# Third unit's h by twenty block products, with w_in's sums made ahead of it

## The chip, the core and the metric

The kernel runs on one core of one Trainium2 chip. The metric is the time of one execution in microseconds (us) on the device. Three runs of the kernel before took 576.93, 576.26 and 574.91 us; the median is 576.26 us. Another execution, taken with the profiler, gave the trace that everything below is read from.

## What is computed

The reference is a gated linear attention over 4 batches, 8 heads, 768 tokens and 48 channels, followed by a two-layer MLP on its output:

```python
for t in range(S):
    state = f[:, :, t, :, None] * state + np.einsum('bhd,bhe->bhde', k[:, :, t], v[:, :, t])
    y[:, :, t] = np.einsum('bhd,bhde->bhe', q[:, :, t], state)
...
x = attn_out.transpose(0, 2, 1, 3).reshape(B * S, H * D)     # 3072 x 384
h = x @ w_in                                                  # 3072 x 2048
g = h * (1.0 / (1.0 + np.exp(-1.702 * h)))
out = g @ w_out                                               # 3072 x 384
```

f is the sigmoid of f_logit. The weights arrive as 64-bit floats and are converted on the chip to 32-bit ones.

## The kernel before

The tokens are cut into twelve units of 256 tokens (n = 0 to 11, three per batch). Each unit goes through attention and then through the MLP. TensorE (PE) works on both at once: a list named fill holds the MLP's matmuls of earlier units, and a plan says after which part of a unit's attention how many of them are issued.

**Attention of a unit.** VectorE (DVE) turns f, q and k into the layout that is needed (turn, line 382; reads raw). GpSimd (POOL) makes products of the decays in a tree (begin_gates, line 457, tile tot; its first one must wait until the states of the unit before have been read from tot). There are six levels: PE makes scores (tile sc, line 466), DVE multiplies the keys and queries X by decays (promote, line 564), ScalarE (ACT) sets copies aside (Kc and Qc, lines 535 and 541), DVE and ACT move the scores out of PSUM into A (lines 507, 516, 526). Two levels share one sc tile, in levels(0), levels(2) and levels(4). Part S adds A times v (line 584), makes the state updates on PE (line 695) and chains the states on DVE (lines 717 to 721, tile st). Part W adds queries times states (line 742), copies y out (yT, line 757) and sends it by DMA to xT (lines 815 and 820), the MLP's input.

**The MLP of a unit, plain form** (mlp_h, line 1173; mlp_o, line 1187). Units 0 and 1 use it in blocks of four of the sixteen 128-row slices of w_in: per slice three matmuls of 128x128 by 128x256, then the activation on ACT; then matmuls with w_out. DVE sums the blocks (line 1243).

**The twenty-product form** (mlp_h20, line 1042). Units 3 to 11 use it. w_in and the unit's x are cut into blocks, and h comes from twenty products of sums of w_in's blocks (WA) by sums of x's blocks (E), four matmuls of 128x128 by 128x128 each (line 1079), in the order WHOLE. The sums of x, twelve, are made on POOL by sums_of_x (line 1037) from xT, after part W. The sums of w_in are made once: some into tiles of their own (sums_of_w, line 1000, names c1, c2, c3, c4, p4, p6, p12, p15, p16), nine in place over w_in's blocks (sums_in_place: k and p3, p1, p14, p7, p19, p9, p5, p11). DVE adds products that meet in one block of h (line 1107), ACT copies (lines 1086, 1098) and activates (1094, 1109). The w_out side of units 2 to 11 is a scheme of seven products on PE (mlp_o7, line 937; results o_Y, o_W, o_X, o_Z) that uses sums of w_out's quarters, T[1] to T[4] (line 851, DVE), and sums of g (lines 872 to 881, DVE).

**Unit 2 before** has h in the plain form, 48 matmuls of 256 columns in groups of four slices, last group first. After each group, when its slices of w_in are read, sums_in_place(r) overwrites blocks of w_in. So w_in's sums are complete only for unit 3.

**What sets the order.** Up to unit 2's attention every engine's order is the program's own (manual_schedule over all engines, closed by fill_order.close()); after it only PE and POOL keep it, and a scheduler orders DVE, ACT and SP, held back where issue_after names an instruction. PLAN and HOLES are strings of steps run after each part of units 1 to 3, or inside a level: f issues the next item of fill, c one step of a weight's conversion (lines 241, 248, 251), p begins a conversion (ACT, line 252), w fetches a pair of weight slices by DMA from SP, s runs one of chores, a list of sums, and k is a matmul that does nothing. From unit 4 on merge shares out the fill. xT tiles and the sums E rotate through three buffers of one tag.

Some deciding lines of the kernel before:

```python
if n > N_FILL:                      # N_FILL = 2
    sums_of_x(n)
...
if n > N_FILL:
    return mlp_h20(n, g, before) + o
...
for r in reversed(range(NGR)):
    items += mlp_h(n, range(r * FG, (r + 1) * FG), by_block)
    if r:
        items.append((0, lambda r=r: sums_in_place(r), 0))
```

Of the kernel before, what the change touches and what calls it, by code (L numbers as in the profile page):

```python
# [23 lines left out]
def kernel(  # L24
# [248 lines left out]
            state["done"] += 2  # L273


    HOLES = {(N_FILL, 0): "c", (N_FILL, 1): "cccffcfcw", (N_FILL, 2): "fcp", (N_FILL, 3): "cfcf", (N_FILL, 4): "fcwwff", (N_FILL, 5): "c"}

    def convert_in(n, l):

# [73 lines left out]
    def attention(n):  # L353
# [19 lines left out]
        def turn(j, outs, fn=None, pieces=None):  # L373

            if n >= N_FILL and not (n == N_FILL and j in BY_PE):
                for f in (1, 0):
                    out = outs(f)
                    at, step = (0, 1) if f else (HALF - 1, -1)
                    with ExitStack() as order:
                        if j == 2 and f == 0 and n % 2 == 0 and "sum" in copied:  # L380
                            order.enter_context(tc.issue_after(copied["sum"].ins))
                        copied["turned"] = nc.vector.transpose(  # L382
                            view(out, at, [[HALF, NP], [step, R4], [R4 * step, 32]]),
                            by_half[:, j, f].rearrange("p a (j d) -> p (a j) d", j=R4)[:, :, :32],
                        )
# [339 lines left out]
        def _():  # L725
# [101 lines left out]


    HF, HC = NFF // 2, DM // 2
    T = {}  # L830
# [4 lines left out]
    def sums_of_b():  # L835
# [9 lines left out]
        made = count()  # L845
# [37 lines left out]
    def mlp_o7(n, g):  # L883
        a = lambda i, j: lambda f: g[j][:, f, i * G:(i + 1) * G]
        s = lambda i: lambda f: g["S"][:, f, i * G:(i + 1) * G]
        b = lambda i, j: lambda f: quarter(w_out, i, j)[:, f]
        T_ = lambda i: lambda f: T[i][:, f] if i < 4 else T[4](f)
        t = {}
        left, right = slice(0, HC), slice(HC, DM)

# [83 lines left out]
    def sums_of_w(names):  # L974

        for name in names:
            if name == "p16":
                WA[name] = wp.tile([P, 2 * DM], F32, tag="s", name="N_p16", bufs=1)[:, :FG * P]
            else:
                WA[name] = const.tile([P, FG * P], F32, name=f"N_{name}")  # L980
            WA[name] = WA[name].rearrange("p (t x) -> p t x", x=2 * P)
        first = (
            ("c3", "a30", "", "a32"), ("p15", "a21", "+", "a31"), ("c2", "a11", "+", "a12"), ("p6", "c2", "+", "a22"),
            ("p6", "p6", "", "c3"),
        )
        second = (
            ("c1", "a01", "+", "a02"), ("c4", "a02", "", "a00"), ("p12", "a11", "", "c4"), ("p4", "c1", "-", "a30"),
            ("p12", "p12", "+", "a10"), ("p16", "a20", "", "a21"), ("p12", "p12", "+", "a20"), ("p16", "p16", "", "a22"),
            ("p15", "p15", "", "p4"),
        )  # L990
        for out, x, op, y in first if "c3" in names else second:
            yield lambda x=(out, x, op, y): sum_of_w(nc.vector if x[2] == "-" else nc.gpsimd, *x)

    def sum_of_w(engine, out, x, op, y):

        if op == "-":
            with tc.issue_after(copied["promoted"].ins):
                engine.scalar_tensor_tensor(WA[out], WA[x], -1.0, WA[y], op0=ALU.mult, op1=ALU.subtract)
        else:
            engine.tensor_tensor(WA[out], WA[x], WA[y], ALU.add if op else ALU.subtract)  # L1000

    def sums_in_place(r):

        while chores:
            chores.pop(0)()
        pool, ve = nc.gpsimd, nc.vector
        for engine, out, at, x, op, y in {
            3: (
                (pool, "k", "a02", "a02", "+", "a30"), (pool, "p3", "a02", "a11", "", "k"), (ve, "p7", "a01", "a11", "", "c3"),
                (ve, "p11", "a00", "a00", "", "c1"),  # L1010
            ),
            2: (
                (pool, "p14", "a10", "a10", "", "c2"), (ve, "p19", "a12", "c2", "-", "a20"), (ve, "p9", "a11", "c4", "", "a11"),
            ),
            1: ((pool, "p1", "a32", "a21", "+", "c3"), (ve, "p5", "a31", "a31", "", "c3")),
        }[r]:
            WA[out] = WA[at]
            sum_of_w(engine, out, x, op, y)

    def sums_of_x(n):  # L1020

# [20 lines left out]
    def mlp_h20(n, g, before):  # L1042
# [68 lines left out]
        def begin():  # L1111
            for half in range(2):
                g[half] = g_tile(f"g_{n}_{half}", width(n))
            free = lanes["o"]
# [44 lines left out]
    def mlp_h(n, ffs, g):  # L1159
        t = {}  # L1160

        def one(ff, c):
            if c == 0:
                if ff % FG == 0:

                    if not halves:
                        new = g_tile(f"g_{n}_{ff}")
                        halves.extend((new[:, :FG], new[:, FG:]))
                        g["tile", ff // HF] = new
                    g[ff // FG] = halves.pop(0 if n < N_FILL else -1)  # L1170
                t["ph"] = bank([P, U], f"h_{n}_{ff}")
            ph = t["ph"]
            nc.tensor.matmul(  # L1173
# [26 lines left out]
    def mlp_unit(n, fill):  # L1200
# [15 lines left out]
        by_block = {}  # L1216

        def end():

            g[0], g[1] = (by_block["tile", i] for i in range(2))  # L1220
            sums_of_a(n, g)
            lanes["o"] = [next(turns) % 4 for _ in range(4)]
        items = []
        for r in reversed(range(NGR)):
            items += mlp_h(n, range(r * FG, (r + 1) * FG), by_block)
            if r:
                items.append((0, lambda r=r: sums_in_place(r), 0))
        return items + [(0, end, 0)] + o

    sums = {}  # L1230

# [92 lines left out]
    def follow_steps(steps):  # L1324

        for step in steps:
# [7 lines left out]
            elif step == "w":  # L1334
                fetch_weights()
            elif step == "s":
                for job in chores[:1]:
                    chores.remove(job)
                    job()
# [21 lines left out]
    def opening():  # L1361
# [16 lines left out]
        load_v(0)  # L1378
        load_raw(1, 1)
        fetch_weights()  # L1380
        for l in range(NL):
            chosen[:] = [2, 3][l % 2:][:1]
            level(l)
# [12 lines left out]
        for l in range(NL - 1):  # L1396
            evacuate(l)
            if l == 1:
                units[0][3]()
                fetch_weights()  # L1400
        chosen[:] = [2, 3, 2, 3]
        next_q()
        begin_pair(1)
# [4 lines left out]
        for _ in range(NOP):  # L1408
# [5 lines left out]
    FIRST = 'k'  # L1414
    PLAN = {
        3: (
            "ffffffsfffsfff", "fffsf", "ffffs", "fffsfsfssfffff", "s", "f", "ffsffffff", "ffffffffff", "fffffsssf",
        ),
        1: (
            "cccwcccwkkkkk", "kkkcf", "cfccwf", "fcffcwffcffcf", "ffcc", "f", "cwc", "fcc", "ff", "cff", "", "f",  # L1420
            "wffwfffff",
        ),
        2: (
            "ffffff", "fcfff", "fcffffccswfwpfcsf", "cfc", "ccfcffscsffcf", "ffffsffffffff", "f", "fffcffsffff",
        ),
    }
    fill += mlp_blocks((0, 0)) + mlp_blocks((0, 1))
# [8 lines left out]
    while chores:  # L1436
        chores.pop(0)()
# [12 lines left out]
    
# [34 lines left out]
```

## Time and profile before

| | before |
|---|---|
| median of three runs | 576.26 us |
| the profiled execution: its time, its span | 575.35 us, 573.6 us |
| mean granted TensorE clock | 1.000 |
| PE, PEld busy | 563.7, 516.7 us |
| DVE, ACT, POOL busy | 441.2, 291.7, 144.5 us |
| share of PE in the chain that ended last | 90% |

The span runs from the first to the last instruction; 1.75 us of the profiled execution lie around it. PE counts matmuls and PEld weight loads, which overlap. Every 32-bit matmul of the program stands in the trace as two matmuls, so unit 2's 48 matmuls are 96 records. The ends of matmuls are modelled, so this text takes the time of a matmul from one start to the next. A line of the timeline has the start, the time to the end of the merged group, engine, line, operation and tiles, the count, and in brackets the idle time ahead and what ended it.

### The profile page before, as it was taken

To read this page: it belongs to the slowest core of one execution; us is meant where nothing else is said; L and a number is where in the kernel's file an instruction comes from. 1 tells how busy PE (TensorE), PEld (TensorE's weight loads), DVE (VectorE), ACT (ScalarE), POOL (GpSimd) and SP (SyncE) were. 2 spreads that over 40 slices of the span, in tenths; PEclk is the share of its full clock that TensorE was granted. 3 is DMA by queue.
4 is the path that set the end of the run, shared out by engine and by line. 5 is a ranking of instruction groups with operands and counts; after the bars stand their busy time and mean duration, and the time that the engine had idled before them with its cause. 6 is when DMAs were issued, how large, how long until landed. Compare 5 with 4: busy or idle time off the path is not lost.

```text
span 573.6 us, 18612 instructions
## 1 busy us (share of the span) xinstructions
PE 563.7 (98%) x7876; PEld 516.7 (90%) x7876; DVE 441.2 (77%) x695; ACT 291.7 (51%) x592; POOL 144.5 (25%) x227
## 2 busy tenths in 40 slices
PE   8899999999999999999999999999999999999997
PEld 7767777786899999999999999999999999999996
DVE  2899688988997786887887888886888886462294
ACT  4755553432553573564564564564564573543440
POOL 4030220419451601601601601601501601303000
PEclk9999999999999999999999999999999999999999
DMA  7869595932362452363453353453362121001000
GB/s 180 207 183 228 138 261 133 246 79 77 84 163 68 120 139 57 85 172 76 109 129 71 97 130 88 113 127 71 97 158 44 49 57 30 30 2 29 29 1 28
DMA packets 85939, 60.01 MB, mean 105 GB/s; under 512 B 33441, under 2 KB 77633, under 8 KB 85857
## 3 DMA queue, kind: packets, MB, share of 16 engines
q1 hardware_dynamic: 85328, 58.21, 40.3%
q8 instruction: 62, 1.02, 0.8%
q10 hardware_dynamic: 529, 0.62, 0.4%
q14 instruction: 20, 0.16, 0.1%
HBM read 45.16 MB, written 8.91 MB: 94 GB/s over the span
## 4 chain that ended last, share of the span: by engine, by line
PE 90%; DMA 3%; DVE 2%; ACT 2%; issue 1%; SPq 1%; ACTq 0%; DVEq 0%
PE h L1079 28%; PE o_Y L937 14%; PE o_Z L937 9%; PE h L1173 9%; PE sc L466 6%; PE o L1187 6%; PE o_X L937 5%; PE o_W L937 4%; PE y L584 2%; PE y L742 2%; PE t L394 2%; PE sc L695 2%; DMA xT<-yT 1%; DVE X L564 1%; DMA bits<-in_moe_w_in_dram 1%
## 5 line engine op out<-in xcount | busy, mean ns | idle before, releaser
L564 DVE TENSOR_TENSOR X<-X,tot 128x1024 f32<-128x1024 f32 x50 | 69.0, 1381 | 40.7 <-PE sc L466 35.1
L535 ACT COPY Kc<-X 128x512 f32<-128x512 f32 x72 | 48.3, 671 | 85.6 <-DVE X L564 71.0
L1079 PE MATMUL h<-E,w_in 128*128 128x128 f32 (+1 forms) x648 | 82.6, 276 | 0.0
L1079 PEld LDWEIGHTS h<-E,w_in 128*128 128x128 f32 x648 | 77.1, 192 | 0.5
L1107 DVE TENSOR_TENSOR g<-g,h 128x512 f32<-128x512 f32 (+1 forms) x92 | 55.4, 628 | 25.9 <-PE h L1079 18.0
L1037 POOL TENSOR_TENSOR E<-xT 128x128 f32<-128x128 f32 (+1 forms) x36 | 16.0, 454 | 231.0 <-DMA xT<-yT 231.0
L1173 PE MATMUL h<-xT,w_in 128*128 128x256 f32 x288 | 65.6, 382 | 0.2 <-DMA xT<-yT 0.2
L1173 PEld LDWEIGHTS h<-xT,w_in 128*128 128x128 f32 x288 | 53.8, 190 | 9.3 <-DMA xT<-yT 0.6
L1109 ACT ACTIVATE g<-g 128x512 f32<-128x512 f32 (+1 forms) x70 | 40.3, 588 | 34.1 <-DVE g L1107 34.1
L937 PE MATMUL o_Y<-T,S 128*128 128x192 f32 x320 | 57.6, 329 | 0.0
L937 PEld LDWEIGHTS o_Y<-T,S 128*128 128x128 f32 x320 | 52.3, 190 | 0.5
L1187 PE MATMUL o<-w_out,g 128*128 128x384 f32 x128 | 44.3, 492 | 0.0
L1098 ACT ACTIVATE g<-h 128x512 f32<-128x512 f32 (+1 forms) x70 | 37.0, 550 | 12.9 <-PE h L1079 11.0
L382 DVE STREAM_TRANSPOSE X<-raw 128x512 f32<-128x512 f32 x38 | 40.9, 1115 | 1.5 <-PE y L742 1.0
L526 DVE COPY_PREDICATED A<-masks,sc 128x256 f32<-128x256 uint32 (+1 forms) x98 | 41.9, 503 | 0.0
L757 ACT COPY yT<-y 48x256 f32<-48x256 f32 (+1 forms) x66 | 22.0, 369 | 30.0 <-PE y L742 29.5
L1079 PE MATMUL h<-E,N_c 128*128 128x128 f32 (+1 forms) x288 | 37.1, 275 | 0.0
L1187 PEld LDWEIGHTS o<-w_out,g 128*128 128x128 f32 x128 | 23.6, 190 | 14.6 <-issue 0.7
L1079 PEld LDWEIGHTS h<-E,N_c 128*128 128x128 f32 x288 | 35.1, 192 | 0.2 <-DVE osb L897 0.2
L466 PE MATMUL sc<-X,Kc 48*64 48x64 f32 x1344 | 28.3, 220 | 3.0 <-ACT Kc L535 1.2
L1177 ACT ACTIVATE g<-h 128x256 f32<-128x256 f32 x48 | 17.7, 382 | 25.5 <-PE h L1173 25.2
L466 PEld LDWEIGHTS sc<-X,Kc 48*64 48x64 f32 x1344 | 24.1, 134 | 7.3 <-ACT Kc L535 3.1
(132 smaller groups left out, 1103.4 us busy)
## 6 DMA issues: line engine op xcount, KB each, us to landing
bits<-in_moe_w_out_dram SPq DMA_DIRECT2D x8, 768.0 KB
raw<-in_f_logit_dram SPq DMA_DIRECT2D x48, 96.0 KB
raw<-in_k_dram SPq DMA_DIRECT2D x48, 96.0 KB
bits<-in_moe_w_in_dram SPq DMA_DIRECT2D x8, 576.0 KB
raw<-in_q_dram SPq DMA_DIRECT2D x44, 96.0 KB
k_tok<-z SPq DMA_DIRECT2D x64, 64.0 KB
kt<-k_tok SPq DMA_DIRECT2D x16, 256.0 KB
out_dram<-osb SPq DMA_DIRECT2D x20, 192.0 KB
```

Of the source, the lines that this page charges most:

```text
L382: copied["turned"] = nc.vector.transpose(view(out, at, [[HALF, NP], [step, R4], [R4 * step, 32]]), by_half[:, j, f].rearrange("p a (j d) - ...
L466: nc.tensor.matmul(t["sc"][h][g * HS:(g + 1) * HS, a, s, :], lhsT=t["Kc", l][rows(h), x:x + HS], rhs=rhs(h, a, g), start=True, stop=True,)
L526: moved = nc.vector.copy_predicated(out=view(A, c * HALF + at, dims), mask=mask.bitcast(U32), data=got)
L535: nc.scalar.copy(c.rearrange("p (n two m) -> p n two m", two=2, m=m), view(X, KF * SLOT, [[2 * m, SLOT // (2 * m)], [(KR - KF) * SLOT + m, ...
L564: done = nc.vector.tensor_tensor(x, x, y, ALU.mult)
L937: nc.tensor.matmul(t[name], lhsT=lhs(f), rhs=rhs(f), start=(new and i == 0), stop=(i == HF - 1), skip_group_check=True,)
L1079: nc.tensor.matmul(ph[:, t], lhsT=WA[a][:, f // 2, f % 2 * P:(f % 2 + 1) * P], rhs=E[n][b], start=(root and t == 0), stop=not goes_on, ski ...
L1098: nc.scalar.activation(to, ph, AF.Copy, scale=float(sign))
L1107: copied["sum"] = nc.vector.tensor_tensor(to, to, part, ALU.add if sign > 0 else ALU.subtract)
L1109: nc.scalar.activation(to, to, AF.Gelu_apprx_sigmoid)
L1173: nc.tensor.matmul(ph, lhsT=w_in[:, ff // 2, c, ff % 2 * P:(ff % 2 + 1) * P], rhs=xTs[n][:, c, :], start=(c == 0), stop=(c == NK - 1))
L1187: nc.tensor.matmul(t["po"], lhsT=g[ff // FG][:, ff % FG, tt * P:(tt + 1) * P], rhs=w_out[:, ff, :], start=(ff == ffs[0]), stop=(ff == ffs[ ...
```

## The change

Unit 2's h is made by the twenty products as well. For that:

- sums_of_x is called for every unit that reaches it: unit 2, and unit 0 too, for which nothing reads them. (Unit 1 returns ahead of that line.)
- All of w_in's sums must stand ahead of unit 2's h. The sums c1, c4 and p12 follow the first five on POOL within unit 2's plan. Four in place (k, p3, p1, p14) go to POOL and five (p7, p19, p9, p5, p11) to DVE. p4 (DVE) and p15's last step (POOL) come behind these, p16's two steps (POOL) behind unit 2's sums of x.
- The sums T of w_out no longer wait for the turn of unit 3's k.
- The plans of units 1 to 3 and HOLES are laid anew. In PE's order, unit 2's sc of levels 2 and 3 comes ahead of five w_out matmuls of unit 1 instead of behind them, part W of unit 2 ahead of three w_out matmuls, 24 instead of 34 of unit 2's w_out matmuls lie between part W of unit 3 and unit 3's first product, and the rest of the order hardly differs. The opening's DMA order is the same; the DMA of weight pair 9 goes ahead of unit 2's v, that of pair 11 behind unit 3's f_logit.

```diff
-    HOLES = {(N_FILL, 0): "c", (N_FILL, 1): "cccffcfcw", (N_FILL, 2): "fcp", (N_FILL, 3): "cfcf", (N_FILL, 4): "fcwwff", (N_FILL, 5): "c"}
+    HOLES = {(N_FILL, 0): "ccc", (N_FILL, 1): "c", (N_FILL, 3): "cpccfwwff", (N_FILL, 4): "ccsw", (N_FILL, 5): "f"}
...
-            if n > N_FILL:
-                sums_of_x(n)
+            sums_of_x(n)
...
         def sub(*x):
-            with ExitStack() as order:
-                if next(made) < 2:
-                    order.enter_context(tc.issue_after(copied["turned"].ins))
-                nc.vector.tensor_tensor(*x, ALU.subtract)
+            summed.append(nc.vector.tensor_tensor(*x, ALU.subtract))
...
-        if op == "-":
-            with tc.issue_after(copied["promoted"].ins):
+        with ExitStack() as order:
+            if engine == nc.vector:
+                order.enter_context(tc.issue_after(copied.get("promoted", copied["state"]).ins))
+            if op == "-":
                 engine.scalar_tensor_tensor(WA[out], WA[x], -1.0, WA[y], op0=ALU.mult, op1=ALU.subtract)
+            else:
+                engine.tensor_tensor(WA[out], WA[x], WA[y], ALU.add if op else ALU.subtract)
...
+    def sums_in_place(engine):
+
+        if engine == nc.gpsimd:
+            for out, at in (("p7", "a01"), ("p19", "a12"), ("p5", "a31"), ("p9", "a11"), ("p11", "a00")):
+                WA[out] = WA[at]
+            sums = (
+                ("k", "a02", "a02", "+", "a30"), ("p3", "a02", "a11", "", "k"), ("p1", "a32", "a21", "+", "c3"),
+                ("p14", "a10", "a10", "", "c2"),
+            )
         else:
-            engine.tensor_tensor(WA[out], WA[x], WA[y], ALU.add if op else ALU.subtract)
...
+            sums = (
+                ("p7", "a01", "a11", "", "c3"), ("p19", "a12", "c2", "-", "a20"), ("p9", "a11", "c4", "", "a11"),
+                ("p5", "a31", "a31", "", "c3"), ("p11", "a00", "a00", "", "c1"),
+            )
...
-        if n > N_FILL:
-            return mlp_h20(n, g, before) + o
...
+        return mlp_h20(n, g, before) + o
...
     chores += [*sums_of_w(("c3", "p15", "c2", "p6"))]
+    more = [lambda: sums_of_w(("c1", "c4", "p12")), lambda: sums_of_w(("p4", "p16"))]
     follow(2, fill, PLAN[2])
...
-    while chores:
-        chores.pop(0)()
+    by_pool, by_ve, rest = [*sums_in_place(nc.gpsimd)], [*sums_in_place(nc.vector)], [*more.pop()()]
+    for x in (*by_pool, *by_ve[:2], *rest[:2]):
+        x()
...
-    of_b = [*sums_of_b()]
-    for x in sums_of_w(("c1", "c4", "p12", "p4", "p16")):
-        chores += of_b[:1] + [x]
-        del of_b[:1]
-    chores += of_b
+    chores += by_ve[2:] + rest[2:] + [*sums_of_b()]
     follow(3, fill, PLAN[3])
```

More of the change, by code (lines that the diff above doesn't have):

```diff
@@ L381, in turn @@
                             order.enter_context(tc.issue_after(copied["sum"].ins))
-                        copied["turned"] = nc.vector.transpose(
+                        nc.vector.transpose(
                             view(out, at, [[HALF, NP], [step, R4], [R4 * step, 32]]),
@@ L829 @@
     HF, HC = NFF // 2, DM // 2
-    T = {}
+    T, summed = {}, []
     def quarter(w, i, j, ffs=slice(0, HF)):
@@ L886, in mlp_o7, with T_, block @@
         b = lambda i, j: lambda f: quarter(w_out, i, j)[:, f]
-        T_ = lambda i: lambda f: T[i][:, f] if i < 4 else T[4](f)
+        def T_(i):
+            def block(f):
+                assert len(summed) == 8
+                return T[i][:, f] if i < 4 else T[4](f)
+            return block
         t = {}
@@ L986, in sums_of_w @@
         second = (
-            ("c1", "a01", "+", "a02"), ("c4", "a02", "", "a00"), ("p12", "a11", "", "c4"), ("p4", "c1", "-", "a30"),
-            ("p12", "p12", "+", "a10"), ("p16", "a20", "", "a21"), ("p12", "p12", "+", "a20"), ("p16", "p16", "", "a22"),
-            ("p15", "p15", "", "p4"),
-        )
-        for out, x, op, y in first if "c3" in names else second:
+            ("c1", "a01", "+", "a02"), ("c4", "a02", "", "a00"), ("p12", "a11", "", "c4"),
+            ("p12", "p12", "+", "a10"), ("p12", "p12", "+", "a20"),
+        )
@@ L992, in sums_of_w @@
+        third = ("p4", "c1", "-", "a30"), ("p15", "p15", "", "p4"), ("p16", "a20", "", "a21"), ("p16", "p16", "", "a22")
+        for out, x, op, y in first if "c3" in names else third if "p16" in names else second:
             yield lambda x=(out, x, op, y): sum_of_w(nc.vector if x[2] == "-" else nc.gpsimd, *x)
     def sum_of_w(engine, out, x, op, y):
-        if op == "-":
-            with tc.issue_after(copied["promoted"].ins):
+        with ExitStack() as order:
+            if engine == nc.vector:
+                order.enter_context(tc.issue_after(copied.get("promoted", copied["state"]).ins))
+            if op == "-":
@@ L998, in sum_of_w @@
                 engine.scalar_tensor_tensor(WA[out], WA[x], -1.0, WA[y], op0=ALU.mult, op1=ALU.subtract)
-        else:
-            engine.tensor_tensor(WA[out], WA[x], WA[y], ALU.add if op else ALU.subtract)
-    def sums_in_place(r):
-        while chores:
-            chores.pop(0)()
[L1006 to L1018, printed above, removed]
+            else:
+                engine.tensor_tensor(WA[out], WA[x], WA[y], ALU.add if op else ALU.subtract)
@@ new lines, in sums_in_place, with job @@
+    def sums_in_place(engine):
[6 more added lines that the diff above has]
+            )
+        else:
+            sums = (
+                ("p7", "a01", "a11", "", "c3"), ("p19", "a12", "c2", "-", "a20"), ("p9", "a11", "c4", "", "a11"),
+                ("p5", "a31", "a31", "", "c3"), ("p11", "a00", "a00", "", "c1"),
+            )
+        for out, at, x, op, y in sums:
+            def job(out=out, at=at, x=x, op=op, y=y):
+                WA[out] = WA[at]
+                sum_of_w(engine, out, x, op, y)
+            yield job
@@ L1113, in begin @@
                 g[half] = g_tile(f"g_{n}_{half}", width(n))
-            free = lanes["o"]
+            free = lanes.get("o") or [next(turns) % 4 for _ in range(4)]
             lanes["h"] = [free[x] for x in ((1, 2, 0, 3) if groups == 1 else (1, 2, 3, 0))]
@@ L1169, in one @@
                         g["tile", ff // HF] = new
-                    g[ff // FG] = halves.pop(0 if n < N_FILL else -1)
+                    g[ff // FG] = halves.pop(0)
                 t["ph"] = bank([P, U], f"h_{n}_{ff}")
@@ L1213, in mlp_unit @@
             del fill[-2 * HF:]
-        if n > N_FILL:
-            return mlp_h20(n, g, before) + o
[L1216 to L1228, printed above, removed]
+        return mlp_h20(n, g, before) + o
     sums = {}
@@ L1336, in follow_steps @@
             elif step == "s":
+                if not chores and more:
+                    chores.extend(more.pop(0)())
                 for job in chores[:1]:
@@ L1380, in opening @@
         fetch_weights()
+        fetch_weights()
         for l in range(NL):
@@ L1416 @@
         3: (
-            "ffffffsfffsfff", "fffsf", "ffffs", "fffsfsfssfffff", "s", "f", "ffsffffff", "ffffffffff", "fffffsssf",
-        ),
-        1: (
-            "cccwcccwkkkkk", "kkkcf", "cfccwf", "fcffcwffcffcf", "ffcc", "f", "cwc", "fcc", "ff", "cff", "", "f",
-            "wffwfffff",
-        ),
-        2: (
-            "ffffff", "fcfff", "fcffffccswfwpfcsf", "cfc", "ccfcffscsffcf", "ffffsffffffff", "f", "fffcffsffff",
+            "sssssfcfffsssfffffsffff", "sfffffff", "", "", "fffpfsffsffsffffffffffffffff", "f", "f",
+            "ffffffffffffffffffff", "ffff",
+        ),
+        1: (
+            "cccwcccwkkkkk", "kkkcf", "cfccwf", "fcffcwffcffcf", "ffcc", "f", "cwc", "fcc", "cfff", "", "pw", "fff",
+            "wffffff",
+        ),
+        2: (
+            "fffff", "ffcfffpcff", "sfcfffcfcsfcpccffwwfcs", "", "fffscfff", "scffscfssfscffffcfffffffcf", "",
+            "fpfffff",
         ),
```

4 lines of the change are left out of this document (removed).

## The prediction

> **What bounds the kernel now.** I read the page's first part, then PE's waits from 60 to 200 us, then the timelines of PE, DVE and POOL around unit 2's h.
>
> ```profile
> PE 563.7 (98%) x7876; PEld 516.7 (90%) x7876; DVE 441.2 (77%) x695; ACT 291.7 (51%) x592; POOL 144.5 (25%) x227
> ```
> ```profile
> PE sc L466 <- DVE A L526: 0.6, 1, 0.6
> PE sc L466 <- ACT Kc L535: 0.4, 1, 0.4
> ```
>
> PE is the bound: in 140 us it waits 1.0 us in all. So time goes if PE gets less work and nothing new is late. The stretch that the change touches has little room elsewhere (windows; behind the window and its length stand the busy us of PE, PEld, DVE, ACT and POOL):
>
> ```profile
> 40.00:50.00 10.00, 10.00 (x98) 7.14 (x97) 9.43 (x20) 5.37 (x10) 0.00 (x0) 1.00 1.04 248
> 120.00:130.00 10.00, 10.00 (x120) 8.62 (x110) 9.76 (x15) 3.77 (x10) 2.76 (x3) 1.00 0.46 99
> 130.00:140.00 10.00, 10.00 (x154) 6.47 (x153) 9.04 (x11) 3.78 (x9) 9.61 (x9) 1.00 0.25 61
> 150.00:160.00 10.00, 10.00 (x49) 8.79 (x48) 9.97 (x13) 5.00 (x13) 4.50 (x3) 1.00 0.40 94
> ```
>
> From 120 to 170 us DVE is over 90% busy. It, not PE, will say what the change is worth. The timelines of PE, then DVE, then POOL:
>
> ```profile
> 85.27 0.69 PE L466 MATMUL sc<-Qc,Kc 48*64 48x64 f32 x32 [0.59 <-DVE A L526]
> ```
> ```profile
> 147.83 0.69 PE L466 MATMUL sc<-X,Kc 48*64 48x64 f32 x32 [0.42 <-ACT Kc L535]
> 148.45 17.10 PE L1173 MATMUL h<-xT,w_in 128*128 128x256 f32 x78
> 165.39 0.81 PE L937 MATMUL o_Y<-w_out,g 128*128 128x192 f32 x4
> ```
> ```profile
> 195.88 3.74 PE L1079 MATMUL h<-E,w_in 128*128 128x128 f32 x32
> 199.45 1.06 PE L1079 MATMUL h<-xT,w_in 128*128 128x128 f32 x8
> ```
> ```profile
> 133.21 1.75 DVE L564 TENSOR_TENSOR X<-X,tot 128x1024 f32<-128x1024 f32 x1 [0.96 <-PE sc L466]
> ...
> 136.47 2.07 DVE L564 TENSOR_TENSOR X<-X,tot 128x1024 f32<-128x1024 f32 x1
> ...
> 142.20 1.48 DVE L564 TENSOR_TENSOR X<-X,tot 128x1024 f32<-128x1024 f32 x1 [1.03 <-PE sc L466]
> ...
> 144.92 2.20 DVE L564 TENSOR_TENSOR X<-X,tot 128x1024 f32<-128x1024 f32 x1
> ```
> ```profile
> 127.08 1.04 POOL L457 TENSOR_TENSOR tot<-F 128x512 f32<-128x512 f32 x1 [16.62 <-DVE st L720]
> 128.20 4.16 POOL L457 TENSOR_TENSOR tot<-tot 128x256 f32<-128x256 f32 x4
> ...
> 144.78 1.27 POOL L1000 TENSOR_TENSOR N_p<-N_p,N_p 128x512 f32<-128x512 f32 x1
> ```
>
> To be seen: PE's wait at 147.83 hangs on the multiplication at 144.92 (with its copy Kc behind it); DVE has only two gaps ahead of that, both waits for PE; POOL's tree for unit 3 waits for unit 2's states, and its sums run until 146.05.
>
> **PE's work.** Out go 48 plain matmuls, 96 records of 256 columns; 78 of them take 165.39 - 148.45 = 16.94 us, 0.217 each: -20.8 us. In come 80 matmuls, 160 records of 128 columns; 32 of them take 199.45 - 195.88 = 3.57 us, 0.112 each: +17.9 us. Nothing else on PE is added or removed. Sum **-2.9 us**, all on the path.
>
> **The wait at 85.27.** The sc tile is free only when the earlier scores are moved out. DVE now does that before the conversion of weight pair 9 (0.56 and 0.96 us) and with two multiplications straight after each other, but PE also asks 3.2 us sooner (five w_out matmuls of 0.646 us, ten records, now follow). Pair 9's DMA, which DVE waited 0.90 us for at 76.99, is issued ahead of unit 2's v. Bounds: the wait of 0.6 goes, or grows to about 2 if POOL's c2 and p6 run beside DVE there. I take **-0.3**, nearer to the first, as DVE moves some 4 us forward.
>
> **The opening.** POOL makes twelve sums for unit 0 that nobody reads, from about 38.8 us, when xT has landed (PE's first h), for 7.3 us (the sums of unit 3: 184.15 to 191.49). POOL was idle from 40 to 50, so its queue loses nothing, but DVE is 94% busy there. Beside POOL, DVE's conversion (L251) takes 1.92 instead of 0.95 us and L564 up to 2.20 instead of 1.22. PE's scores at 43.88 and 53.27 had their copies 1.2 and 1.4 us early, and DVE idles 1.8 us at 57. Bounds 0 and +1.2; I take **+0.3**, as the margin covers most.
>
> **DVE up to unit 2's states** (end at 127.39). Added ahead of them: three T sums (3 x 0.95) and a conversion (0.95 to 1.63) that ran behind them, 4 to 4.5 us; and POOL's c1, c4, p12 (five of 1.3 to 2.3 us), which ran from 132.6, now run beside DVE at about 109 to 118. Against that, DVE idled there 1.6 us for ACT, 0.9 and 2.0 us for PE. The last sum of unit 1's w_out products still cannot start before 116.6, and from there DVE has a sum, a conversion, two turns, two T, the multiplication, a T and the states: 0.5 + 1.0 + 1.9 + 1.9 + 1.2 + 0.9 + 3.1 = 10.5 us, to 127.1 alone and 129 beside POOL. States about **1.0 us late**. Part W of unit 2 on PE, 131.0 before, is due at 129.04 (six records of 0.323 less ahead of it) and needs all but the last state: covered, by 0.7 us.
>
> **DVE from there to the scores at 147.83.** Before, a T trio and the conversion (5.0 us) and gaps of 2.0 us; now p19 and p4 (0.71 and 0.73), p7, p9, p5 and p11 (1.1 to 1.75 each, 1.33 mean of the four rows of that line), with p4 out of its old place: +6.0 -5.0, less most of the gaps. So the multiplication that began at 144.92 begins some 0.3 us later than before, from 1.3 earlier (no gap left to close but PE's scores, which come two w_out matmuls sooner) to 2.5 later. The copy Kc is ready at about 148.2. PE is there sooner: the three plain slices ahead (3.9 us) are three products (2.7), so it could begin at 145.9. Wait 2.3 us instead of 0.6, the 0.6 being the 0.42 us and the scores' slow end: **+1.7**. Here goes most of the gain; the bounds are +0 and +4.
>
> **POOL ahead of the first product.** From the states' end: the tree 5.3 us, k, p3, p1, p14 5.8 (1.63, 1.59, 1.28, 1.28), p15 1.27: E may start at 140.8 with the states 1 us late, 142.1 at the mean of 1.68 us that POOL's eight sums took from 132.61 to 146.05. xT of unit 2 has landed by then: its last DMA was issued at 137.4, now two us sooner. In unit 3's run the fourth sum ended 2.8 us and the sixth 4.7 us after the first began; products take 0.89 us each, so the first product may start 1.9 us behind E without a halt: 142.7 to 144.0. PE gets there at 142.65. This wait lies inside the one above, since the same scores follow after three products: +0. If the states came 2 us later still, it would not.
>
> **Unit 3.** Between part W's end and the first product lie 24 instead of 34 w_out matmuls: 13.3 - 3.3 = 10.0 us. E started 8.2 us after part W's end (175.92 to 184.15) and needs 1.9: 10.1. **+0.2**, bounds 0 and +1. DVE has to make 10 additions (0.686 each) for unit 2's h, where six operand sums stood: about +1 us over 46, not on the path, as the states are asked for 7.8 us after their matmuls instead of 3.9.
>
> **Sum**: -2.9 - 0.3 + 0.3 + 1.7 + 0.2 = -1.0 us. Against the profiled execution (573.6 of span and 1.75 around it, 575.35) that is 574.4; the median of the runs, 576.26, lies 0.9 above that execution. I take the middle: **574.8**.
>
> **The port rule.** The row: L564 beside POOL costs 0.3 to 1.0 us more, by less than a POOL sum's 1.27 us. The Trainium skill, page "SBUF — State Buffer", section "Who interferes with whom", says that a DVE instruction with two SBUF inputs and a GpSimd one that reads SBUF block each other, the later one wholly. By that each of the five moved POOL sums could hold DVE for its full length; the rows have it smaller here, but the direction speaks against the change, and the third case below is its mechanism.
>
> **The cases.** (1) As summed, DVE late by a little at unit 3's scores: 574.8, from 574.5 to 578.0, chance 0.42. (2) The plan hides it all: DVE's idle time takes the added work, the waits at 85.27 and 147.83 go, and PE keeps its 2.9 us: 576.26 or 575.35 less 2.9 to 3.4, 572.0 to 573.4; with half of that lost, up to 574.5. For it: DVE's gaps of 4.5 us between 98 and 117; against it: 97% from 120 to 130. Chance 0.40. (3) Slower: POOL's sums beside DVE's conversions and T sums. Rows from 104 to 111: L248 1.25 for 0.55, L241 1.63 for 0.55, L251 1.92 for 0.95, some 3.4 us in 6.2 us of POOL. Five sums of 1.7 us at that rate are 4.7 us on DVE; 1 is in the sum above, the rest would move the states to 131 or later, part W waits 1.5 us, E comes 3 us later, and Kc near 151: 575.8 + 2.7 = 578.5. It decides the sign when that Kc comes later than about 149.2, 1.0 us behind my estimate. Chance 0.18. That the products replace nothing is excluded: the built order has them.
>
> **Chances and range.** A measurement of this kernel can tell about 0.3%, 1.7 us. Faster than 574.5: 0.40; within: 0.42; above 578.0: 0.18. The range takes in the whole of (2) and (3)'s price: 572.2 to 578.6; case (1)'s own is 574.5 to 578.0.
>
> **What would show it.** Right: L1173 only 192 records, L1079 160 more; PE waits for Kc (L535) at unit 3's last scores by 1.5 to 3 us, and hardly for E; the states of unit 2 end between 127.5 and 129.5. Wrong: a PE wait for POOL's E or for the states above 1 us, a wait at about 81 to 89 us for A, or in the opening at 43 to 54 for Kc; or PE without a wait in that whole stretch, which is case (2).

## The result and the profile after

The changed kernel is slower. In twelve runs beside twelve of the kernel before, its median is 577.86 us against 575.51 us; the ratio is 1.0038, with a 95% interval of 1.0026 to 1.0049. A second measurement, beside other runs of the kernel before, gave 578.21 against 575.71 us, a ratio of 1.0048 (1.0032 to 1.0064). The forecast was 574.8 us, with a range of 572.2 to 578.6 us. The measured times lie inside that range, and inside the interval of the likeliest case, but the direction was wrong: faster was forecast, and a slower kernel was the third case, with a chance of 0.18. The profiled execution of the changed kernel took 578.97 us, its span is 577.0 us. The line numbers below are the changed kernel's; up to line 780 they are those of before (466 is sc, 560 and 564 the multiplications X, 526 the move to A, 535 Kc), behind it h of the products is 1085, plain h 1179, the w_out matmuls 1193, sums of w_in 1003, sums of x 1043, activations of plain h 1183. An edit that adds a line moves the lines behind it by one or two.

The page's first part of the changed kernel, then PE's waits from 40 to 60 us and from 60 to 200 us (us in all, times, longest):

```profile
PE 562.1 (97%) x7940; PEld 516.8 (90%) x7940; DVE 448.9 (78%) x705; ACT 295.1 (51%) x594; POOL 162.6 (28%) x251
```
```profile
PE o L1193 <- ACT g L1183: 0.8, 1, 0.8
PE sc L466 <- DVE X L560: 0.4, 1, 0.4
```
```profile
PE sc L466 <- DVE A L526: 1.5, 2, 0.8
PE sc L466 <- ACT Kc L535: 1.0, 1, 1.0
PE h L1179 <- ACT g L1183: 0.6, 1, 0.6
PE h L1179 <- DVE X L382: 0.4, 1, 0.4
```

PE has less to do, as forecast. But where the kernel before waited for 1.0 us between 60 and 200 us, the changed one waits for 3.5 us there, and 1.2 us more from 40 to 60 us, where before had no such wait. Two of the stretches shown of before, now (columns as there):

```profile
40.00:50.00 10.00, 9.58 (x98) 6.93 (x96) 9.97 (x17) 3.76 (x8) 8.58 (x12) 1.00 1.08 250
130.00:140.00 10.00, 10.00 (x160) 7.49 (x159) 7.26 (x12) 4.53 (x12) 7.75 (x9) 1.00 0.38 75
```

From 40 to 50 us POOL, which was idle, is busy for 8.58 us, and DVE has no gap left. From 130 to 140 us DVE, which had been busy for 9.04 us, now idles for 2.7 us in the middle of the stretch that was to be too full for it. These two rows led to the two main experiments.

A sum in what follows is made of **lost time**: how much later a matmul of PE starts after the one ahead of it than is usual for these two shapes in the same trace. It lies 0.01 to 0.24 us above the wait that the timeline shows in brackets. From 60 to 200 us it is 1.3 us in the kernel before.

### The profile page after: what moved, and what is told of

Same layout as the page of the kernel before. It is cut to its first block, busy times and chain, and to the rows that moved or that the text cites. A ratio compares the mean times of both kernels' runs of the same rounds, so it can differ in the third digit from the quotient of the medians.

```text
span 577.0 us, 18797 instructions
## 1 busy us (share of the span) xinstructions
PE 562.1 (97%) x7940; PEld 516.8 (90%) x7940; DVE 448.9 (78%) x705; ACT 295.1 (51%) x594; POOL 162.6 (28%) x251
## 4 chain that ended last, share of the span: by engine, by line
PE 80%; DVE 4%; DMA 2%; ACT 2%; issue 1%; SPq 0%; DVEq 0%; ACTq 0%
PE h L1085 31%; PE o_Y L938 14%; PE o_Z L938 9%; PE sc L466 5%; PE o_X L938 5%; PE o_W L938 4%; PE h L1179 4%; PE o L1193 2%; DVE X L564 2%; PE y L584 2%; PE y L742 2%; PE sc L695 2%; DMA bits<-in_moe_w_in_dram 1%; DMA xT<-yT 1%; DVE A L526 1%
## 5 line engine op out<-in xcount | busy, mean ns | idle before, releaser
L1043 POOL TENSOR_TENSOR E<-xT 128x128 f32<-128x128 f32 (+1 forms) x44 | 26.1, 602 | 249.2 <-DMA xT<-yT 219.7
L1085 PE MATMUL h<-E,w_in 128*128 128x128 f32 (+1 forms) x720 | 91.8, 276 | 0.0
L1085 PEld LDWEIGHTS h<-E,w_in 128*128 128x128 f32 x720 | 85.7, 192 | 0.6
L1113 DVE TENSOR_TENSOR g<-g,h 128x512 f32<-128x512 f32 (+1 forms) x101 | 61.3, 632 | 25.3 <-PE h L1085 15.8
L1115 ACT ACTIVATE g<-g 128x512 f32<-128x512 f32 (+1 forms) x77 | 44.7, 592 | 38.1 <-DVE g L1113 38.0
L1104 ACT ACTIVATE g<-h 128x512 f32<-128x512 f32 (+1 forms) x77 | 41.2, 554 | 13.4 <-PE h L1085 12.7
L1179 PE MATMUL h<-xT,w_in 128*128 128x256 f32 x192 | 44.5, 383 | 1.0 <-ACT g L1183 0.6
L1179 PEld LDWEIGHTS h<-xT,w_in 128*128 128x128 f32 x192 | 35.7, 190 | 7.6 <-ACT g L1183 1.0
L1085 PE MATMUL h<-E,N_c 128*128 128x128 f32 (+1 forms) x320 | 41.5, 276 | 0.0
L1085 PE MATMUL h<-xT,N_p 128*128 128x128 f32 (+1 forms) x240 | 32.1, 275 | 0.0
```

Source lines behind the costliest of these rows:

```text
L1085: nc.tensor.matmul(ph[:, t], lhsT=WA[a][:, f // 2, f % 2 * P:(f % 2 + 1) * P], rhs=E[n][b], start=(root and t == 0), stop=not goes_on, ski ...
L1104: nc.scalar.activation(to, ph, AF.Copy, scale=float(sign))
L1113: copied["sum"] = nc.vector.tensor_tensor(to, to, part, ALU.add if sign > 0 else ALU.subtract)
L1115: nc.scalar.activation(to, to, AF.Gelu_apprx_sigmoid)
L1179: nc.tensor.matmul(ph, lhsT=w_in[:, ff // 2, c, ff % 2 * P:(ff % 2 + 1) * P], rhs=xTs[n][:, c, :], start=(c == 0), stop=(c == NK - 1))
```

## The experiments

All ratios are to the kernel before, measured on the same chip in the same session; 0.1% is 0.58 us. Each had five rounds, but for three that had three. The first four rows are one session, the next three a second, the last three a third on another chip, so rows of different sessions are compared through the kernel before alone.

| kernel | ratio | 95% interval | median us |
|---|---|---|---|
| changed, again | 1.0048 | 1.0032 to 1.0064 | 578.21 |
| changed, without unit 0's sums | 1.0011 | 1.0000 to 1.0023 | 576.02 |
| before, with unit 0's sums | 1.0009 | 0.9996 to 1.0023 | 576.49 |
| without unit 0's sums, unit 1's old plan | 1.0052 | 1.0038 to 1.0066 | 578.32 |
| without unit 0's sums, p9 last (three rounds) | 0.9995 | 0.9980 to 1.0010 | 575.25 |
| without unit 0's sums, front sums late (three rounds) | 1.0041 | 1.0030 to 1.0051 | 577.49 |
| without unit 0's sums, h inside the levels (three rounds) | 1.0009 | 1.0000 to 1.0019 | 576.21 |
| p9 last, h inside, two more w_out matmuls | 0.9968 | 0.9955 to 0.9982 | 573.65 |
| the same, p1 and p14 behind E | 0.9954 | 0.9942 to 0.9966 | 572.76 |
| changed, p9 last alone | 1.0017 | 1.0003 to 1.0031 | 576.05 |

### Unit 0's unread sums

Theory A was that the twelve sums of x that nobody reads hold up DVE in the opening; theory B that the new order of units 1 to 3 costs the time; theory C that the opening's waits belong to one execution. Four kernels, the first one unchanged:

> The changed kernel as it is, beside the three below. Theory A (unit 0's unread sums of x on GpSimd hold up VectorE in the opening) and theory B (the new order of units 1 to 3 makes TensorE wait at about 72, 83, 93 and 144 us) both expect 2.0 to 2.7 us more than the kernel before, and the same waits at about 42 and 50 us as in the first profile. Theory C (the opening's wait of 2.0 us without a releaser at 27 us and the lower granted clock from 20 to 40 us belong to the one profiled execution) expects a wait of about 0.9 us there and a granted clock of 1.00 in this profile.

The changed kernel without the sums:

```diff
-            sums_of_x(n)
+            if n >= N_FILL:
+                sums_of_x(n)
```

> The changed kernel without unit 0's twelve sums of x, which nothing reads; the output is the same. Theory A: the waits at about 42 (X, line 560) and 50 us (the activation g) go, and it is 1.1 to 1.5 us faster than the changed kernel, 0.9 to 1.3 us slower than the kernel before. Theory B alone: it is within 0.4 us of the changed kernel, as the waits from 72 us on stay.

The kernel before with them:

```diff
-            if n > N_FILL:
+            if n != N_FILL:
                 sums_of_x(n)
```

> The kernel before with unit 0's twelve unread sums of x added, nothing else. Theory A: 1.1 to 1.5 us slower than the kernel before, with a wait for Kc, X or g between 40 and 54 us. Theory B: within 0.4 us of the kernel before.

Without the sums the changed kernel is 0.37% faster (1.0048 to 1.0011), 2.1 us; against the first measurement, 1.0038, it is 1.6 us. Theory A had 1.1 to 1.5 us. In the kernel before, the same sums cost 0.09%, 0.5 us, with an interval that holds nothing as well as 1.3 us: less than theory A expected. The trace shows how. The timelines of POOL, DVE, ACT and PE of the changed kernel (start, time, engine, line, operation; in brackets the idle time ahead and what ended it):

```profile
39.92 1.92 POOL L1043 TENSOR_TENSOR E<-xT 128x128 f32<-128x128 f32 x2 [6.66 <-DMA xT<-yT]
```
```profile
44.01 1.81 DVE L560 TENSOR_TENSOR X<-X,tot 128x512 f32<-128x512 f32 x2
...
49.23 1.28 DVE L560 TENSOR_TENSOR X<-X,tot 128x512 f32<-128x512 f32 x2
```
```profile
49.94 0.62 ACT L535 COPY Kc<-X 128x512 f32<-128x512 f32 x1 [2.96 <-DVE X L560]
50.47 0.38 ACT L1183 ACTIVATE g<-h 128x256 f32<-128x256 f32 x1
```
```profile
50.90 2.85 PE L1193 MATMUL o<-w_out,g 128*128 128x384 f32 x8 [0.82 <-ACT g L1183]
```

Two POOL sums that take 0.87 us elsewhere take 1.92, and DVE's two multiplications beside POOL 1.81 us, where the same pair took 1.29 us in the kernel before. DVE keeps the program's order there: from the pair at 40.58 us to the one at 49.23 us it needs 8.65 us, from 38.51 to 45.61 us in the kernel before 7.10. So this X comes late though it takes its usual 1.28 us, the copy Kc waits for it at the head of ACT's queue, the activation g stands behind the copy, and PE waits for g, which has nothing to do with X. The same wait is in the second execution of the changed kernel (1.03 us) and, smaller, in the kernel before with the sums (0.54 us); in the kernel without them there is none between 38 and 68 us. Lost time over all waits behind 40 us falls from 5.8 to 4.6 us, 1.2 us. What the ratio has beyond that is within its interval.

Theory C was half right. In the second execution the wait without a releaser at 27 us is 1.34 us instead of 1.98, and the granted clock stays 1.00 from 20 to 40 us.

### Unit 1's plan

```diff
-"cfff", "", "pw", "fff", "wffffff"
+"ff", "cff", "", "f", "wffwfffff"
```

> The changed kernel without unit 0's sums of x and with unit 1's plan as in the kernel before (the plans of units 2 and 3 stay new). Theory B: the waits at about 72 and 83 us, 1.35 us together, go and it is 1.0 to 1.5 us faster than the kernel without unit 0's sums. Theory A says nothing of them: if the waits come from the plan of unit 2 (levels 0 and 1) or from unit 0's sums, the time stays within 0.4 us of that kernel.

The waits of 0.9 and 0.8 us at 80 and 90 us do go, but one of 2.75 us comes, and the kernel is 0.41% slower than without this edit, against theory B's 1.0 to 1.5 us of gain. PE's timeline and the window behind it (length, PE, granted clock, DMA share, GB/s):

```profile
77.39 1.14 PE L466 MATMUL sc<-X,Kc 48*64 48x64 f32 x32 [2.75 <-ACT Kc L535]
```
```profile
75.00:80.00 5.00, 2.60 (x36) 0.74 1.08 269
```

In that kernel DVE idles 1.86 us for ACT's step of a conversion ("bits", line 252), and then does the rest of the conversion, 2.9 us beside two POOL sums, ahead of the multiplication that Kc needs. The step p in unit 1's new plan begins that conversion earlier. So the new plans of unit 2 need this part of unit 1's. What unit 1's plan costs by itself this run does not show: the lost time in waits from 70 to 95 us is 3.0 us for 2.3, and the rest of the 0.41% lies in the clock, which was 0.74 here and 0.92 in the next 5 us, 1.7 us of full clock in all. All five runs of this kernel show a granted clock of 0.994 to 0.997.

### p9, and DVE's idle time

```diff
-("p9", "a11", "c4", "", "a11"), ("p5", "a31", "a31", "", "c3"), ("p11", "a00", "a00", "", "c1"),
+("p5", "a31", "a31", "", "c3"), ("p11", "a00", "a00", "", "c1"), ("p9", "a11", "c4", "", "a11"),
```

> The changed kernel without unit 0's sums of x, and with p9 as the last instead of the third of VectorE's five sums in place. In the kernel without unit 0's sums VectorE idles 1.9 us at 134.6 us, as p9 overwrites a block that GpSimd's p3 still reads. Theory D (this idle time is what makes the wait for A at 141 us and lengthens the wait for Kc at 148 us): the idle time goes, the two waits of TensorE, 0.7 and 1.2 us of lost time, fall by 1.0 to 1.5 us together, and the kernel is that much faster than the one without unit 0's sums (no slower than the kernel before). Theory E (VectorE's added work and GpSimd's sums beside it make these waits, wherever p9 stands): within 0.4 us of that kernel.

In the kernel without unit 0's sums, POOL, DVE and PE:

```profile
132.80 3.64 POOL L1004 TENSOR_TENSOR w_in<-w_in 128x512 f32<-128x512 f32 x2
```
```profile
136.48 1.74 DVE L1004 TENSOR_TENSOR w_in<-N_c,w_in 128x512 f32<-128x512 f32 x1 [1.91 <-POOL w_in L1004]
138.13 2.28 DVE L564 TENSOR_TENSOR X<-X,tot 128x1024 f32<-128x1024 f32 x1
```
```profile
141.79 0.69 PE L466 MATMUL sc<-Qc,Kc 48*64 48x64 f32 x32 [0.64 <-DVE A L526]
...
149.37 0.69 PE L466 MATMUL sc<-X,Kc 48*64 48x64 f32 x32 [0.98 <-ACT Kc L535]
```

With p9 last, whose trace has everything ahead of here 1.76 us later:

```profile
136.26 1.15 DVE L1004 TENSOR_TENSOR w_in<-w_in,N_c 128x512 f32<-128x512 f32 x1
```
```profile
142.83 0.69 PE L466 MATMUL sc<-Qc,Kc 48*64 48x64 f32 x32
...
149.49 0.65 PE L466 MATMUL sc<-X,Kc 48*64 48x64 f32 x32
```

p9 overwrites a11, and POOL's p3 reads a11. DVE has its orders in a row, so everything behind p9 waits with it: the next multiplication, the move to A, and so the scores. With p5 in p9's place DVE has no gap, and both waits of PE are gone, 1.9 us of lost time, more than theory D's 1.0 to 1.5. The time fell by 0.16%, 0.9 us, within what the intervals of three rounds leave. The granted clock hides part of it: it was 0.994 to 0.997 in five of the ten runs of this kernel (575.62 to 576.43 us) and 0.999 or 1.000 in the other five (573.67 to 574.89 us), but in eleven of twelve of the kernel without unit 0's sums. Runs of 0.999 and 1.000 alone have medians of 574.34 us (before: 575.35) and 575.91 us (before: 575.49): 1.4 us faster, as theory D has it. In the profile the clock fell at 30 us, ahead of all that the edit moves. The changed kernel as it stands, with this edit alone:

> The changed kernel with p9 last and nothing else; unit 0's unread sums of x stay. Theory D: without VectorE's idle time behind p3 the waits at about 142 and 149 us go, and it is 0.8 to 1.9 us faster than the changed kernel, 0.5 to 1.5 us slower than the kernel before. If the two causes were one, unit 0's sums having delayed everything that follows, it would be within 0.4 us of the changed kernel.

It is 0.21 to 0.31% (1.2 to 1.8 us) faster than the changed kernel's two measurements, and its trace has no wait between 92 and 189 us: theory D holds, and the two causes add up.

### POOL's front sums, and the order of the activations

Two waits stay at 80 and 90 us. In the kernel without unit 0's sums, POOL, DVE, ACT and PE:

```profile
74.91 1.59 POOL L1004 TENSOR_TENSOR N_p<-w_in 128x512 f32<-128x512 f32 x1
83.47 1.52 POOL L1004 TENSOR_TENSOR N_c<-w_in 128x512 f32<-128x512 f32 x1 [6.97 <-DVE w_in L251]
```
```profile
75.30 2.30 DVE L564 TENSOR_TENSOR X<-X,tot 128x1024 f32<-128x1024 f32 x1
...
83.94 2.13 DVE L564 TENSOR_TENSOR X<-X,tot 128x1024 f32<-128x1024 f32 x1
```
```profile
80.17 0.62 ACT L535 COPY Kc<-X 128x512 f32<-128x512 f32 x1 [1.41 <-DVE X L564]
80.69 1.20 ACT L1184 ACTIVATE g<-h 128x256 f32<-128x256 f32 x4
```
```profile
81.12 1.56 PE L1180 MATMUL h<-xT,w_in 128*128 128x256 f32 x6 [0.94 <-ACT g L1184]
...
91.24 0.69 PE L466 MATMUL sc<-Qc,Kc 48*64 48x64 f32 x32 [0.81 <-DVE A L526]
```

The sums are those of before at other times: c3 and p15 began 1.2 to 2.2 us later (73.7 instead of 71.5 us, 74.9 instead of 73.7), c2 and the first step of p6 some 22 us earlier (83.5 and 85.1 instead of 105.4 and 107.4). In the kernel before they ran beside conversions; now p15 and c2 run beside two multiplications that Kc and A wait for (2.30 and 2.13 us, where 1.23 is usual). And four activations stand on ACT behind a copy to Kc. The first experiment holds the five sums back with a copy of one element on POOL from a late conversion (step g):

```diff
-(N_FILL, 4): "ccsw" ... "sfcfffcfcsfcpccffwwfcs"
+(N_FILL, 4): "ccw" ... "fcgssfffcfcsfcpccffwwfcs"
```

> The changed kernel without unit 0's sums of x, and with GpSimd's five sums c3, p15, c2 and p6 held back until a conversion that ends at about 96 us (one element of it is copied on GpSimd ahead of them); before that they ran at 73.7 to 76.5 and 83.5 to 87.2 us. Theory F (these sums, beside VectorE's multiplications of lines 560 and 564 and its conversions, make the waits at 80 and 90 us): VectorE's multiplications there take 1.2 instead of 2.1 to 2.3 us, the waits of 1.1 and 0.9 us fall to 0.7 us or less together, and the kernel is 0.8 to 1.5 us faster than without unit 0's sums. Theory G (they come from the order: the activations stand behind Kc on ScalarE, and fewer w_out matmuls lie ahead of the scores): the waits change by less than 0.5 us.

The waits at 80 and 90 us go, and the multiplications take 1.23 us each: theory F has the cause right. But the kernel is 0.30% slower, for four of the sums now run at 94.6 to 99.9 us, where DVE converts (DVE, POOL, then PE):

```profile
95.81 2.95 DVE L242 TENSOR_SCALAR s<-bits 128x768 int32<-128x768 int32 x1
```
```profile
95.86 1.26 POOL L1005 TENSOR_TENSOR N_p<-w_in 128x512 f32<-128x512 f32 x1
```
```profile
106.27 1.56 PE L1181 MATMUL h<-xT,w_in 128*128 128x256 f32 x6 [1.90 <-ACT kn L649]
```

A step that takes 0.55 us alone took 2.95, and the turn of unit 3's f came 1.8 us later than without the edit. ACT waited 4.22 us for it, with kn and three activations behind it, and PE for those. The wait for A at 143 us grew as well, from 0.64 to 1.60 us. The cost of these sums was not lost by moving them; it fell on what was beside them. The second experiment moves only activations on ACT:

```diff
-(N_FILL, 1): "c",                       2: ("fffff", ...
+(N_FILL, 1): "cf", (N_FILL, 2): "ff",   2: ("ff", ...
```

> The changed kernel without unit 0's sums of x, and with three of unit 1's slices of h issued inside unit 2's levels 0 and 1 instead of behind them: TensorE's order is the same, only ScalarE has their activations ahead of two copies to Kc instead of behind them. Theory G, order on ScalarE: the wait for the activation at 80 us (1.1 us) goes; as VectorE does not get faster by it, the wait for A at 90 us takes most of it (1.5 to 2.0 us instead of 0.9), and the time stays within 0.5 us of the kernel without unit 0's sums. If VectorE itself was held by TensorE there, the 1.1 us are won.

The wait for g goes; 0.29 us for A come in its place, and the wait at 90 us grows from 0.81 to 1.28 us. The time stays (1.0009 for 1.0011). DVE sets the time there, and the wait of PE that was taken away came back at the next things that DVE delivers.

### What lies behind, and a version faster than both

If PE gets two more w_out matmuls ahead of the late scores, the wait at 90 us is covered. The traces said what would be late next: with p9 last, E began at 144.14 and the first product at 145.96 us, 1.8 us behind it, with nothing to spare.

```diff
-"fffff", "ffcfffpcff", "sfcfffcfcsfcpccffwwfcs"
+"ff", "ffcfffpcffff", "scffcfcsfcpccffwwfcs"
```

> The changed kernel without unit 0's sums of x, with p9 last, with three slices of unit 1's h inside unit 2's levels 0 and 1 (as in the run that moved these alone), and with two more w_out matmuls of unit 1 (1.3 us) ahead of unit 2's last scores. Theory H (the waits at 80 and 90 us can be covered, but what follows is bound by GpSimd's chain of unit 3's tree, the sums in place and unit 2's E, which began 1.8 us ahead of the first product with p9 last and left it no margin): the waits up to 92 us fall from 2.5 to 1.2 us or less, a wait for E of 0.7 to 1.5 us comes at unit 2's first products, and the kernel gains 0 to 0.7 us over p9 last alone. Theory I (TensorE's work is the only bound left there): no wait for E, 1.2 to 1.8 us gained.

And with POOL's p1 and p14 behind E, since the products that read them come tenth and eleventh:

```diff
-    for x in (*by_pool, *by_ve[:2], *rest[:2]):
+    for x in (*by_pool[:2], *by_ve[:2], *rest[:2]):
...
-    chores += by_ve[2:] + rest[2:] + [*sums_of_b()]
+    chores += by_pool[2:] + by_ve[2:] + rest[2:] + [*sums_of_b()]
...
-            "sssssfcfffsssfffffsffff", ...
+            "sssssssfcfffsssfffffsffff", ...
```

> As the run beside it with three slices of h moved, p9 last and two more w_out matmuls ahead, and with GpSimd's sums p1 and p14 behind unit 2's sums of x instead of ahead of them. Theory H: E begins 2.9 us sooner if xT has landed, the wait for E goes, and it is 0.7 to 1.5 us faster than that run, 1.0 to 2.0 us faster than the kernel before. Theory I: within 0.4 us of that run. If xT lands only after 141 us, E gains less than 1 us of its start and the wait for it stays in part.

PE's timeline of the first, then POOL's and PE's of the second:

```profile
145.31 1.16 PE L1086 MATMUL h<-E,N_c 128*128 128x128 f32 x8 [0.75 <-POOL E L1044]
```
```profile
138.44 1.83 POOL L1044 TENSOR_TENSOR E<-xT 128x128 f32<-128x128 f32 x2
```
```profile
143.51 1.95 PE L1086 MATMUL h<-E,N_c 128*128 128x128 f32 x16
```

Theory H holds in its waits: 1.3 us of lost time left up to 92 us (1.2 or less expected), 0.75 us for E in the first, and none in the second, in which E begins at 138.44 instead of 142.46 us. The first gained more than expected, 0.27% (1.6 us) over p9 last alone, but about half of that is the clock in the runs with p9 last: by the runs with a granted clock of 0.999 or 1.000 (573.44 us, before 575.19) it is 0.7 us, as expected. The second gained 0.14% (0.8 us) more. At 0.9954 (0.9942 to 0.9966), 2.6 us, it is faster than both kernels: about the 2.9 us that PE was spared, with 1.3 us of lost time left at 75 and 83 us (0.7 at 85 us in the kernel before, and 0.6 at 148).

## Why the prediction was wrong

**PE's work, -2.9 us: right.** From the first record of unit 2's h to o_Y before took 165.39 - 142.74 = 22.65 us; without unit 0's sums 165.28 - 144.92 = 20.36 us. That is 2.3 less, with 0.6 us more lost at Kc in it: 2.9.

**The wait at 85.27, -0.3 us: the step that failed.** The stretch came out 1.85 us worse: 2.5 us lost between 68 and 92 us without unit 0's sums, 0.66 before. The wait that the term names did go (the scores at 82.62 us start at once), but PE lost 1.1 us for g ahead of them, 0.9 us for A at the next scores and 0.5 us at 69 and 74 us. The prediction saw that PE asks earlier and gave a bound of 2 "if POOL's c2 and p6 run beside DVE there", but took the other end, because DVE "moves some 4 us forward". That lead held for the first multiplication only: it began at 75.30 instead of 79.43 us, the fourth at 88.53 instead of 89.07. Of the 3.6 us in between, 3.0 lie in two multiplications and a conversion step beside POOL's sums; with these held back the fourth began at 85.84. The prediction also left out ACT's order, in which g stands behind Kc.

**The opening, +0.3 us: mis-sized.** It measured 0.5 us in the kernel before, 1.3 us (1.0017 to 0.9995) with p9 last, 1.6 to 2.1 us in the changed kernel; the bound was 1.2. The margins of 1.2 and 1.4 us of the copies Kc covered their scores, as argued. But the scores at 40.44 us, whose copy ended only 0.5 us ahead, were left out and waited 0.42 us in the first profile of the changed kernel, and the w_out matmul that waits for an activation behind Kc was not looked at.

**DVE from there to the scores at 147.83, +1.7 us: near in size, wrong in cause.** It measured 1.3 us (0.71 + 1.19 - 0.63). The prediction priced each sum in place at 1.33 us and found DVE too full (the four rows that it names are 0.71 to 1.75 us, 1.22 in the mean, which makes its +6.0 about +5.6). In fact DVE idled 1.9 us, since p9 waits for POOL's p3. That the sums in place overwrite what others read stood in the code; the prediction asked what each sum costs and not what each waits for. With p9 last there is no wait, so that the added DVE work alone would have cost nothing.

**States, E, unit 3: right.** There is no wait for the states, none above 0.2 us for E in the changed kernel, and 0.2 us at unit 3's first products. The states ended at 132.1 us in the changed kernel's first profile, outside the 127.5 to 129.5 that were to show the prediction right, but only because all ahead of them was late: they ended 8.4 us after PE began unit 2's part S, and 8.3 in the kernel before. The front of E was nearer than it looked: it became the bound as soon as 1.2 us of lost time were won ahead of it.

**The sum.** -2.9 + 1.85 + 1.2 + 1.3 + 0.2 = +1.65 us; the measured ratios are 2.2 and 2.8 us, with intervals from 1.5 and 1.8 us. Between the two profiles with a clock of 1.00, the kernel before (575.35 us) and the changed kernel's second (577.08), it is 1.7 us, as in the sum. So the 0.6 to 1.2 us that the ratios have beyond it are not placed. The opening of the profiles does not explain them. The wait without a releaser at 27 us lost 1.0 and 1.1 us in the two profiles of the kernel before and 1.3 to 2.2 us in nine of the ten profiles of changed kernels (in the tenth none), but PE's first h began at 38.57 and 38.89 us in the former and at 38.27 to 39.39 us in eight of the latter: what is lost there is made up ahead of 40 us. In the other two (the first profile of the changed kernel, and p9 last) the granted clock fell behind this wait, and h began at 40.66 and 40.70 us.

**The cases.** The third case named the right mechanism, POOL's sums beside DVE, but at 104 to 118 us, and its time, 578.5 us, came near the measured 577.86 and 578.21 by luck: the waits of part W and for E on which it rests did not come. There DVE was stretched indeed (a conversion's step 1.65 instead of 0.55 us), and PE waited for nothing between 95 and 144 us. It decided at 74 to 87 us and in the opening, where the sums ran beside multiplications. The port rule, which the prediction held to be larger than its rows, bears on those places. The multiplication at 75.30 us lost 1.07 us; POOL's p15, begun ahead of it, ended 1.20 us after its start. The step at 95.81 us lost 2.40 us; it ended 0.4 us behind the second of the two POOL sums, of 1.26 us each, that began 0.05 and 1.27 us behind it. At the rate of these two rows, an estimate, the front sums would have been priced at 1 to 2.4 us for each step that they meet, not at the 0.3 to 1.0 us that the prediction took. The Trainium skill, page "SBUF — State Buffer", section "Who interferes with whom", lets the later of a VectorE and a GpSimd instruction that contend wait for the whole of the other. The first row agrees with it; the second agrees in what is lost, two whole sums, and not in who waits, if the 0.05 us by which the VectorE step began earlier are exact. Two smaller slips: the range begins at 572.2 us, though case (2), which it is said to take in whole, begins at 572.0, and the 97% from 120 to 130 us is 9.76 of 10 us, 98%.

## What to carry to other kernels

A sum on GpSimd is not free because GpSimd is idle: list what VectorE runs beside it, and follow from there to whatever stands behind it on ScalarE's queue, not only to the operand itself. Before pricing an in-place operation, write down who still reads what it overwrites; an order that looks free can put a wait for another engine at the head of a queue. When a wait is taken away, look for the next thing that the same engine delivers, and cover or move that too: here it took four small edits, each shown by the trace of the one before, to turn 0.4% slower into 0.5% faster.

## What was not expected of the hardware

Short gaps on PE can cost more than themselves. After a wait of 1.98 us at 27 us in the changed kernel the granted clock was 0.93 from 25 to 30 and 0.73 from 30 to 35 us, 1.7 us of full clock (between 29.3 and 32.6 us it was 0.50); after 1.89 us at the same place with p9 last 0.66; after 2.75 us at 75 us 0.74 over 75 to 80 and 0.92 over 80 to 85 us. After 1.34 and 1.44 us at 27 us it stayed 1.00, and in the profile with the front sums late also after 1.90 us at 104 us, with PE busy for 30 us ahead of it; six of that kernel's ten runs show a granted clock of 0.996 or 0.997, and where it fell in them is not known. What decides is not shown. The Trainium skill, page "TensorE: Matmul & The Clock Gate", section "Why this matters for your kernels", advises to have no idle gaps of more than about 3 us between bursts of matmuls; here less than 2 us was enough in two profiles, in a stretch with other gaps close by, and not in a third.
